# Softmax attention feeding a gated FFN on one core: key rests shared by four heads, and batch 0 begun with 384 of its 448 queries

## The chip, the core and the metric

The kernel runs on one core of one Trainium2 chip. The metric is the device time of one execution in microseconds (us). A core has TensorE (PE: products; PEld is its loading of the stationary operand), VectorE (DVE), ScalarE (ACT: here exponential, tanh and copies), GpSimd (POOL: here casts, and the issue of the loads that turn float32 into float16) and SyncE (SP: the issue of other transfers). TensorE writes into PSUM, which has eight banks; the other data lie in SBUF. One row of a tile is one partition.

## What is computed

Cut from the reference:

```python
batch, n_heads, seq, head_dim = (8, 12, 448, 64)

def _attn_ref(q, k, v):
    scale = 1.0 / np.sqrt(q.shape[-1])
    scores = scale * np.matmul(q, k.transpose(0, 1, 3, 2))
    scores = scores - np.max(scores, axis=-1, keepdims=True)
    attn = np.exp(scores)
    attn = attn / (np.sum(attn, axis=-1, keepdims=True) + 1e-09)
    return np.matmul(attn, v).astype(np.float32)

def _moe_ref(x, w_gate, w_val, w_out):      # x: (3584, 768), d_ff: 1536
    g = x @ w_gate
    silu = g * (1.0 / (1.0 + np.exp(-g)))
    val = x @ w_val
    return (silu * val @ w_out).astype(np.float32)

# x = attn_out.transpose(0, 2, 1, 3).reshape(B * S, H * D)
```

All inputs and the output are float32; the kernel works in float16 with float32 sums.

## The kernel before

Heads are taken in pairs, 48 in all, six to a batch of 448 queries. Three things are woven together: the attention of one pair (scores, exponential, product with the values), the first FFN layer of a block whose attention is complete ("gate" and "value" products, 12 groups of 6 + 6 a block), and the second FFN layer of the block before. A block is 384 queries (even blocks) or 512 (odd ones); two blocks make two batches. The whole kernel is put into a fixed order by hand (`manual_schedule`), and each engine executes its part in that order.

The 448 keys of a pair lie in four chunks of 112. For a chunk, the scores of both heads are two products with 64 rows each, in the two row halves of TensorE; the result, keys by queries, goes into one score tile of two banks:

```python
ps_s = ...tile_pool(name="ps_s", bufs=3, space=PSUM)    # 3 tiles of two banks
ps_f = ...tile_pool(name="ps_f", bufs=2, space=PSUM)    # 2 tiles of one bank

def qk(pr, c):
    t = qkT[pr]
    s = ps_s.tile([128, 2, 512], FP32, tag="s")
    for hx in range(2):
        nc.tensor.matmul(
            s[:, hx, 0:S],
            lhsT=t[ts(hx, 64), c * P : c * P + 128],
            rhs=t[ts(hx, 64), ds(S + (1 - hx) * D, S)],
            start=True, stop=True)
    e = Es[pr % NE][:, ds(c * EB, 16)].rearrange("p (h b) x -> p h (b x)", h=2)
    nc.scalar.activation(e[:, :, 0:S], s[0:P, :, 0:S], AF.Exp, scale=sm_scale)
```

The product with the values uses blocks of 128 queries as the stationary operand and 64 values plus a column of ones (for the sum) as the moving one, 8 products a chunk, 32 a pair. Queries 384 to 447 of the two heads share one block (`a7[:, 6]`). The seven blocks of a pair fit one bank of `ps_f`. DVE then takes the reciprocal of the sums and multiplies.

```python
def pv_chunk(pr, c):
    if c == 0:
        accs[pr] = ps_f.tile([128, 512], FP32, tag="f", name="acc")
    ...
    for j in range(3):
        for hx in range(2):
            nc.tensor.matmul(a7[:, 2 * j + hx],
                lhsT=e[:, ds(c * EB + 9 * hx + 2 * j, 2)].rearrange(...),
                rhs=vo[:, hx, c, 0 : D + 1], ...)          # 112 rows, 65 columns
    for hx in range(2):
        nc.tensor.matmul(a7[:, 6], ..., rhs=vo[:, hx, c, 0 : D + 1], ...)
    if c < NC - 1:
        return
    nc.vector.reciprocal(r[:, 0:7], a7[:, :, D])
    nc.vector.tensor_tensor(xt[:, 0:n], a7[:, 0:n, 0:D], r[...], ALU.mult)
    ...
```

Q and K must be turned so that the 64 features lie along the rows. For the first 11 pairs TensorE does it (products with a unit matrix, then a DVE copy, `turn`); for the others POOL casts and a DMA transpose turns. The attention results must be turned too (`turn_x`): on TensorE for the first 12 pairs, in a bank of `ps_f` or in the accumulator's own, by DMA transposes for the others.

The start is a loop over the 24 chunks of batch 0, in which no FFN product can run yet. The `dummy` products here and there work on zeros; they only keep TensorE running.

```python
for u in range(FIRST * NC):                 # 6 pairs x 4 chunks
    pr, c = divmod(u, NC)
    qk(pr, c)
    if u == 1:
        dummy(1); turn(); dummy(1)
    ...
    elif u >= 6 and c == 2:
        prep(pr + 2)()                      # q and k of a later pair
    if c == 1:
        for w in wq.pop(pr, []):            # loads; first FFN weights with pair 0
            emit(w)
    if u in CAT: copy_v(...)
    if u in XAT: turn_x(...)
    for _ in range(...):
        if u >= 5 and pieces[0][0] * NC + pieces[0][1] <= u - 3:
            piece()                         # pv_chunk of an earlier chunk
```

After that comes the body, a list of steps: two or three chunks of scores, the products with the values for one pair, then as many FFN groups as are due.

```python
for x, (chunks, todo) in enumerate(plan):
    for pr, c in chunks:
        qk(pr, c)
    ...
    for _, p0 in todo:
        pv(p0)                              # 4 chunks, 32 products
    ...
    for y in range(nf): run_fv()            # gate 6, tanh, value 6
    for _ in range(no): run_o()             # second layer: 12 products
    ...
    while turns:
        turn_x(turns.pop(0))
```

A gate group takes a score tile of `ps_s`, a value group and a second-layer group a bank of `ps_f`. The last part of the output is evicted in two halves of 192 columns:

```python
for ch, oh in steps:
    last = last_block and ch == n // 128 - 1
    ...
    if last and oh:
        parts = [(OH, OH // 2), (OH + OH // 2, OH // 2)]
```

Of the kernel before, what the change touches and what calls it, by code (L numbers as in the profile page):

```python
# [19 lines left out]
NPE = 11  # L20
# [3 lines left out]
WIDE = 8  # L24
XPE = 12
NE = 4
NX = 6
NV = 5
VS = 9
EB = 15  # L30
# [3 lines left out]
def kernel(  # L34
# [24 lines left out]
    MQ = S - D  # L59
# [13 lines left out]
    load_table("exp_and_others")  # L73

# [7 lines left out]
    ps_f = ctx.enter_context(tc.tile_pool(name="ps_f", bufs=2, space=PSUM))  # L82

    Es = [consts.tile([P, NC * EB + 1, D], FP16, name=f"E{i}") for i in range(NE)]
    Xts = [consts.tile([128, 7, D], FP16, name=f"xt{i}") for i in range(NX)]
    Xrs = [consts.tile([D, 128], FP16, name=f"xr{i}") for i in range(3)]
    Vts = [consts.tile([P, 2, NC, D + 2], FP16, name=f"vo{i}") for i in range(NV)]
    vraw = consts.tile([P, VS, 2, NC, D], FP16, name="vraw")
# [11 lines left out]
    wo = [consts.tile([128, NFB, OH], FP16, name=f"wo{i}") for i in range(2)]  # L100
# [5 lines left out]
    def dummy(n):  # L106
        wp = ps_f.tile([128, 512], FP32, tag="f", name="wp")
        for _ in range(n):
            nc.tensor.matmul(wp[:], lhsT=warm[:, 0:128], rhs=warm[:], start=True, stop=True)  # L109

    def load_qk32(pr):
        rq = raws.tile([P, 2, NC, D], FP32, tag="rq", bufs=RB)
        rk = raws.tile([P, 2, NC, D], FP32, tag="rk", bufs=RB)
        for dst, src in ((rq, q), (rk, k)):
            nc.sync.dma_start(dst[:], src[0, 2 * pr : 2 * pr + 2].rearrange("h (p c) d -> p h (c d)", c=NC))
        raw[pr] = (rq[:], rk[:])
# [3 lines left out]
    def load_qk16(pr, n=2):  # L120
        h0 = 2 * (pr % 2) if pr >= 14 else 0
        if h0 == 0:
            q16 = raws.tile([P, 4, NC, D], FP16, tag="rq", bufs=RB, name="q16")
            k16 = raws.tile([P, 4, NC, D], FP16, tag="rk", bufs=RB, name="k16")
            pairbuf[:] = [q16, k16]
        q16, k16 = pairbuf
        for dst, src in ((q16, q), (k16, k)):
            flat = src.rearrange("b h s d -> (b h) s d")[2 * pr : 2 * pr + 2 * n]
            nc.gpsimd.dma_start(dst[:, ds(h0, 2 * n)], flat.rearrange("h (p c) d -> p h (c d)", c=NC))  # L129
        for i in range(n):  # L130
            h = h0 + 2 * i
            raw[pr + i] = (q16[:, h : h + 2], k16[:, h : h + 2])

    def load_v(pr, n=1):
        b, h = divmod(2 * pr, H)
        nc.gpsimd.dma_start(  # L136
            vraw[:, ds(pr % VS, n)].rearrange("p r h c d -> p (r h) (c d)"),
            v[b, h : h + 2 * n].rearrange("h (p c) d -> p h (c d)", c=NC),
        )
# [4 lines left out]
    def load_w(kind, i):  # L144
        if kind == "o":
            src = moe_w_out[:, ts(i, OH)].rearrange("(f p) m -> p f m", p=128)
            dst = wo[i]
        else:
            src = (moe_w_gate if kind == "g" else moe_w_val)[:, ts(i, DF // 4)].rearrange(
                "(t a p) m -> t p a m", p=128, t=2  # L150
            )
            for t in range(2):
                nc.gpsimd.dma_start(wgv[kind, i][:, ts(t, NCB // 2), :], src[t])
            return
        nc.gpsimd.dma_start(dst[:], src)

    def prep(pr):
        rq, rk = raw[pr]
        if pr == 0 or pr >= NPE:
            qk16 = attp.tile([P, 2, NC, 2, D], FP16, tag="qk16", bufs=3)  # L160
            for t, src in enumerate((rq, rk)):
                dst = qk16[:, 1 - t].rearrange("p c h d -> p h c d")
                if pr == 0:
                    nc.vector.tensor_copy(dst[:, 0], src[:, 0])
                    nc.scalar.activation(dst[:, 1], src[:, 1], AF.Copy)
                else:
                    nc.gpsimd.tensor_copy(dst, src)  # L167
        qkT[pr] = attp.tile([128, 2 * S + D], FP16, tag="qkT", name="qkT", bufs=5)
        if pr >= NPE:
            nc.sync.dma_start_transpose(  # L170
                qkT[pr][:, 0 : 2 * S].rearrange("p (c q) -> p c q", q=P),
                qk16[:].rearrange("p t c h d -> p (t c h d)"),
            )
            nc.sync.dma_start_transpose(
                qkT[pr][:, 2 * S :].rearrange("p (c q) -> p c q", c=1),
                qk16[0:D, 1, 0].rearrange("p h d -> p (h d)"),
            )
            return None

        def turn0():  # L180
            for t in range(2):
                tp = ps_s.tile([128, 2, 512], FP32, tag="s", name="tp")
                for c in range(NC):
                    for hx in range(2):
                        nc.tensor.matmul(
                            tp[ts(hx, 64), c // 2, ds(c % 2 * P, P)],
                            lhsT=qk16[:, 1 - t, c, hx],
                            rhs=ident[0:P, 0:P],
                            start=True,
                            stop=True,  # L190
                        )
                dst = qkT[pr][:, ts(1 - t, S)].rearrange("p (a x) -> p a x", a=2)
                nc.vector.tensor_copy(dst[:, 0], tp[:, 0, 0 : 2 * P])
                nc.scalar.activation(dst[:, 1], tp[:, 1, 0 : 2 * P], AF.Copy)
                if t == 0:
                    tq = tp
            nc.vector.tensor_copy(qkT[pr][:, 2 * S :], tq[:, 0, 0:D])

        def turn():
            if pr < FIRST + 2:  # L200
                tp = ps_s.tile([128, 2, 1024], FP16, tag="s", name="tp")[:, 0]
            else:
                tp = ps_f.tile([128, 1024], FP16, tag="f", name="tp")
            for i in range(2 * NC + 1):
                t, c = (1 - i // NC, i % NC) if i < 2 * NC else (0, 0)
                for hx in range(2):
                    src = raw[pr][t][:, hx, c, :]
                    nc.tensor.transpose(tp[ts(hx, 64), ts(i, P)], src, ident[0:P, 0:P])  # L208
            nc.vector.tensor_copy(qkT[pr][:], tp[:, 0 : 2 * S + D])  # L209

        return turn if pr else turn0

    def qk(pr, c):
        t = qkT[pr]
        s = ps_s.tile([128, 2, 512], FP32, tag="s")
        for hx in range(2):
            nc.tensor.matmul(  # L217
                s[:, hx, 0:S],
                lhsT=t[ts(hx, 64), c * P : c * P + 128],
                rhs=t[ts(hx, 64), ds(S + (1 - hx) * D, S)],  # L220
# [3 lines left out]
        e = Es[pr % NE][:, ds(c * EB, 16)].rearrange("p (h b) x -> p h (b x)", h=2)  # L224
        nc.scalar.activation(e[:, :, 0:S], s[0:P, :, 0:S], AF.Exp, scale=sm_scale)  # L225

    def qk_half(pr, half, between=None):
# [414 lines left out]
```

The softmax here doesn't subtract the row's maximum and nothing guards it: scores larger than these inputs give would overflow.

## Time and profile before

Three runs of the kernel before took 453.17, 453.20 and 453.62 us. The profiled execution has a span of 451.7 us; TensorE had a mean granted clock of 0.998 of full speed.

| stage | from, to (us) | what runs |
|---|---|---|
| start | 0 to 29.8 | attention of batch 0; loads of q, k, v and the first weights |
| body | 29.8 to 446.6 | FFN, with the attention of the other 42 pairs up to about 380 us |
| tail | 446.6 to 451.7 | last eviction and output |

| group | count | mean of one |
|---|---|---|
| exponential of a score tile, 2 x 448 columns (ACT) | 192 | 919 ns |
| tanh of a gate group, 384 / 512 columns (ACT) | 48 / 48 | 496 / 598 ns |
| gate and value products, 384 / 512 columns (PE) | 576 / 576 | 326 / 379 ns |
| second-layer products, 384 / 192 columns (PE) | 660 / 24 | 326 / 246 ns |
| score products, 448 columns on 64 rows (PE) | 384 | 355 ns |
| products with the values, 65 columns on 112 rows (PE) | 1536 | 193 ns |

How to read it: the page gives busy time by engine, then the span in 40 slices with a digit of tenths for each, then the chain of work that ended last. The durations of TensorE's products overlap[...]; the mean of one is therefore not its price. What a product costs in a row is the difference of the starts. A table of stretches of time shows which engine is full in which stage.

### The profile page before, as it was taken

Reading aid. Unit: us, or ns where it says so; the run is one execution under the profiler, and the core shown is the slowest. Engines: PE = TensorE matmul, PEld = TensorE weight load, DVE = VectorE, ACT = ScalarE, POOL = GpSimd, SP = SyncE. Lnnn points to the kernel's source line nnn. Section 1 sums busy time; section 2 is a strip of 40 time slices with the busy share of each in tenths; the row PEclk is TensorE's granted clock in tenths of the full one; section 3 lists DMA queues with packets and bytes.
Section 4 is the critical chain, followed back from the end, with each engine's and each line's share of the span. In section 5 each row is a group of like instructions: output and inputs, shape, how many; then the busy total and the mean of one; then the engine's idle time right before and its main releaser. Section 6 shows DMA issues by size and latency. Waiting matters only on the chain.

```text
span 451.7 us, 9871 instructions
## 1 busy us (share of the span) xinstructions
PE 441.9 (98%) x4024; PEld 247.0 (55%) x4024; DVE 201.6 (45%) x447; ACT 238.8 (53%) x350; POOL 141.8 (31%) x228
## 2 busy tenths in 40 slices
PE   8999999999999999999999999999999999999995
PEld 3655565545455556454555656545455666544563
DVE  3666562456654434455443534353453544055300
ACT  6965666566746465554554546644555462222221
POOL 8755715927642225252313405330100000000000
PEclk9999999999999999999999999999999999999999
DMA  9999999999969379874749758772503112200033
GB/s 142 173 200 201 196 172 174 180 209 119 145 93 133 46 129 124 132 120 71 126 74 120 98 78 143 118 105 68 101 20 68 46 46 57 70 2 0 17 100 95
DMA packets 105101, 48.71 MB, mean 108 GB/s; under 512 B 59744, under 2 KB 101600, under 8 KB 105056
## 3 DMA queue, kind: packets, MB, share of 16 engines
q0 software_dynamic: 43392, 23.37, 41.2%
q1 hardware_dynamic: 61664, 24.71, 28.9%
q8 instruction: 31, 0.51, 0.5%
q14 instruction: 14, 0.11, 0.1%
HBM read 47.19 MB, written 11.01 MB: 129 GB/s over the span
## 4 chain that ended last, share of the span: by engine, by line
PE 93%; DVE 3%; ACT 2%; issue 1%; DVEq 0%; ACTq 0%
PE op L371 24%; PE gp L326 23%; PE vp L326 23%; PE s L217 9%; PE acc L243 9%; PE acc L251 2%; ACT E L225 2%; PE tp L208 1%; PE wp L109 1%; DVE t L345 1%; ACT sg L341 1%; DVE qkT L209 0%; DVE xt L264 0%; PE acc L291 0%; DVE hts L348 0%
## 5 line engine op out<-in xcount | busy, mean ns | idle before, releaser
L225 ACT ACTIVATE E<-s 112x896 f16<-112x896 f32 x192 | 162.1, 919 | 27.5 <-PE s L217 27.4
L326 PE MATMUL gp<-X,wg 128*128 128x384 f16 (+1 forms) x576 | 124.7, 352 | 0.0
L326 PE MATMUL vp<-X,wv 128*128 128x384 f16 (+1 forms) x576 | 124.6, 352 | 0.0
L371 PE MATMUL op<-wo,hts 128*128 128x384 f16 (+1 forms) x684 | 116.1, 323 | 0.0
L345 DVE SCALAR_TENSOR_TENSOR t<-sg,gp 128x384 f32<-128x384 f32 (+1 forms) x96 | 59.7, 621 | 121.8 <-ACT sg L341 121.8
L341 ACT ACTIVATE sg<-gp 128x384 f32<-128x384 f32 (+1 forms) x96 | 52.5, 547 | 84.8 <-PE gp L326 83.6
L371 PEld LDWEIGHTS <-hts 128*128 128x128 f16 x684 | 65.5, 98 | 45.9 <-issue 3.9
L326 PEld LDWEIGHTS <-wv 128*128 128x128 f16 x576 | 56.3, 98 | 52.6
L326 PEld LDWEIGHTS <-wg 128*128 128x128 f16 x576 | 53.1, 97 | 45.6 <-issue 1.1
L378 ACT ACTIVATE osb<-op 128x384 f32<-128x384 f32 (+1 forms) x57 | 27.8, 487 | 92.5 <-PE op L371 92.5
L167 POOL COPY qk<-q 112x512 f16<-112x512 f16 x37 | 22.9, 619 | 144.5 <-DMA qkT<-qk 143.1
L348 DVE SCALAR_TENSOR_TENSOR hts<-t,vp 128x384 f16<-128x384 f32 (+1 forms) x96 | 59.6, 621 | 10.0
L243 PEld LDWEIGHTS <-E 112*128 112x128 f16 x1152 | 46.7, 97 | 18.2 <-issue 17.5
L243 PE MATMUL acc<-vo,E 112*128 112x65 f16 x1152 | 53.0, 193 | 1.3 <-DVE vo L142 0.7
L217 PE MATMUL s<-qkT 64*128 64x448 f16 x384 | 50.6, 355 | 0.2
L251 PE MATMUL acc<-vo,E 112*128 112x65 f16 x384 | 42.9, 193 | 0.0
L262 DVE RECIPROCAL R<-acc 128x7 f32<-128x7 f32 x48 | 9.8, 205 | 70.6 <-PE acc L251 70.5
L129 POOL DMA_DIRECT2D k<-in_k_dram x44 | 29.0, 660 | 9.5 <-DMA wo<-in_moe_w_out_dram 7.8
L129 POOL DMA_DIRECT2D q<-in_q_dram x44 | 29.3, 666 | 5.2 <-PE s L217 2.5
L136 POOL DMA_DIRECT2D vraw<-in_v_dram x42 | 28.0, 666 | 8.4 <-DVE vo L142 7.2
L217 PEld LDWEIGHTS <-qkT 64*128 64x128 f16 x384 | 14.5, 94 | 25.8 <-issue 18.6
L264 DVE TENSOR_TENSOR xt<-acc,R 128x384 f16<-128x384 f32 (+1 forms) x48 | 27.6, 574 | 1.7
(41 smaller groups left out, 148.2 us busy)
## 6 DMA issues: line engine op xcount, KB each, us to landing
q<-in_q_dram POOLq DMA_DIRECT2D x41, 112.0 KB, 4.0
k<-in_k_dram POOLq DMA_DIRECT2D x41, 112.0 KB, 4.6
vraw<-in_v_dram POOLq DMA_DIRECT2D x39, 112.0 KB, 4.6
wg<-in_moe_w_gate_dram POOLq DMA_DIRECT2D x8, 288.0 KB, 10.1
wv<-in_moe_w_val_dram POOLq DMA_DIRECT2D x8, 288.0 KB, 10.2
wo<-in_moe_w_out_dram POOLq DMA_DIRECT2D x2, 1152.0 KB, 22.0
out_dram<-osb SPq DMA_DIRECT2D x8, 288.0 KB, 3.0
out_dram<-osb SPq DMA_DIRECT2D x8, 240.0 KB, 3.1
```

The source lines that it names most:

```text
L129: nc.gpsimd.dma_start(dst[:, ds(h0, 2 * n)], flat.rearrange("h (p c) d -> p h (c d)", c=NC))
L136: nc.gpsimd.dma_start(vraw[:, ds(pr % VS, n)].rearrange("p r h c d -> p (r h) (c d)"), v[b, h : h + 2 * n].rearrange("h (p c) d -> p h (c ...
L217: nc.tensor.matmul(s[:, hx, 0:S], lhsT=t[ts(hx, 64), c * P : c * P + 128], rhs=t[ts(hx, 64), ds(S + (1 - hx) * D, S)], start=True, stop=True,)
L225: nc.scalar.activation(e[:, :, 0:S], s[0:P, :, 0:S], AF.Exp, scale=sm_scale)
L243: nc.tensor.matmul(a7[:, 2 * j + hx], lhsT=e[:, ds(c * EB + 9 * hx + 2 * j, 2)].rearrange("p b x -> p (b x)"), rhs=vo[:, hx, c, 0 : D + 1] ...
L251: nc.tensor.matmul(a7[:, 6], lhsT=e[:, ds(c * EB + 6 + hx, 2)].rearrange("p b x -> p (b x)"), rhs=vo[:, hx, c, 0 : D + 1], start=False, st ...
L326: nc.tensor.matmul(dst[:, 0:n], lhsT=wslice(kind, fb, cb), rhs=X[kk][:, cb, ds(c0, n)], start=(cb == 0), stop=(cb == NCB - 1),)
L341: nc.scalar.activation(sg[:, 0:n], gp[:, 0:n], AF.Tanh, scale=0.5)
L345: nc.vector.scalar_tensor_tensor(t1[:, 0:n], sg[:, 0:n], 1.0, gp[:, 0:n], ALU.add, ALU.mult)
L348: nc.vector.scalar_tensor_tensor(hts[:, fb, 0:n], t1[:, 0:n], 0.5 * HS, vp[:, 0:n], ALU.mult, ALU.mult)
L371: nc.tensor.matmul(op[:, 0:w], lhsT=hts[:, fb, ts(ch, 128)], rhs=wo[oh][:, fb, ds(m0 - oh * OH, w)], start=(fb == 0), stop=(fb == NFB - 1),)
L378: nc.scalar.activation(osb[:, ds(m0, w)], op[:, 0:w], AF.Copy, scale=1.0 / HS)
```

## The change

The change does these things together:

- **Keys in three chunks of 128 and a rest of 64.** The rests of both heads of two neighbouring pairs (four heads) share one score tile: four products of 64 rows by 64 columns, one in each quarter of TensorE, then one exponential. Two pairs need 7 score tiles and 7 exponentials instead of 8. For this the loads lay out K and V so that the rest of one head comes in the lower and that of the other in the upper 64 rows.
- **Products with the values** are 4 blocks of queries for each head: 24 products on 128 rows and 8 on the 64 rows of the rests a pair (of the seventh query block, half the result columns are not used). Each head has a bank of its own, so a pair takes two.
- **Batch 0 first for 384 queries.** In the start, each of the six pairs is scored for 384 queries only, which are those of the first FFN block. Its other 64 queries are done for all heads in three score tiles (`qk_rest`, two at the end of the start, one after the first FFN group), one run of products (`pv_rest`) in the next step and one turn (`turn_rest`) in the step after.
- The order of the start is given by a string of letters; TensorE turns q and k for 14 pairs instead of 11 and the results for 18 instead of 12, now in score tiles. Every step of the body has three score tiles. The accumulator of the start has a PSUM pool of its own, given back before the first FFN group.
- q and k of pair 0 are issued by two engines; the second-layer weights come in four parts, later than before.

The core of the diff:

```diff
-NPE = 11
+NPE = 14
-XPE = 12
+XPE = 18
+Q1 = 384
+START = "sstdsdvsstsppppssvtsvppxppsstsppxpspsvtspsppvvpsxsppxpssptsppsppsxx"
 ...
     ps_s = ctx.enter_context(tc.tile_pool(name="ps_s", bufs=3, space=PSUM))
-    ps_f = ctx.enter_context(tc.tile_pool(name="ps_f", bufs=2, space=PSUM))
+    first_acc = ExitStack()
+    psum = {"a": first_acc.enter_context(tc.tile_pool(name="ps_a", bufs=1, space=PSUM))}
 ...
+    def low(pr, hx):
+        return hx == pr % 2
 ...
     def qk(pr, c):
-        t = qkT[pr]
         s = ps_s.tile([128, 2, 512], FP32, tag="s")
+        n = width(pr)                      # 384 for pairs 0 to 5, else 448
+        if c < KR:                         # KR = 3 full chunks
+            t = qkT[pr]
+            for hx in range(2):
+                nc.tensor.matmul(s[:, hx, 0:n], lhsT=t[ts(hx, 64), ts(c + low(pr, hx), 128)],
+                                 rhs=t[ts(hx, 64), ds(NC * 128, n)], start=True, stop=True)
+            e = Es[pr % NE][:, c]
+        else:                              # the rests of pairs pr and pr + 1
+            for hx in range(2):
+                for p in (pr, pr + 1):
+                    lo = low(p, hx)
+                    t = qkT[p]
+                    nc.tensor.matmul(s[ts(1 - lo, 64), hx, 0:n],
+                        lhsT=t[ts(hx, 64), ds(0 if lo else KR * 128 + 64, 64)],
+                        rhs=t[ts(hx, 64), ds(NC * 128, n)], start=True, stop=True)
+            e = Ers[pr // 2 % NR][:]
+        nc.scalar.activation(..., s[:, :, 0:n], AF.Exp, scale=sm_scale)
 ...
+    def pv_mm(pr, hx, c, j):
+        lo = low(pr, hx)
+        ...
+        if c < KR:
+            rows, e, col = slice(0, 128), Es[pr % NE][:, c], c + lo
+        else:
+            rows, e, col = (slice(0, 64), Ers[...], 0) if lo else (slice(64, 128), Ers[...], KR)
+        nc.tensor.matmul(accs[pr][0][hx][:, ts(j, D + 1)], lhsT=e[rows, ds(hx * S + j * 128, 128)],
+                         rhs=Vts[pr % NV][rows, hx, col, 0 : D + 1], ...)
 ...
+    def pv(pr, mid):
+        for hx in range(2):
+            for c in range(KR):
+                pv_piece(pr, c, (hx,))
+            if hx == 0:
+                mid()                      # turn_x of the pair before
+        pv_close(pr)
 ...
         if pr < XPE:
-            tp = accs[pr] if pr < FIRST else ps_f.tile([128, 512], FP32, tag="f", name="xtp")
-            for j in range(3):
+            tp = ps_s.tile([128, 2, 512], FP32, tag="s", name="xtp")[:, 0]
+            for j in range(slots(pr)):     # 3, or 4 from pair 6 on
 ...
                 while l < l0 + 128:
                     b, j = divmod(l, S)
-                    c, p0 = divmod((j + D) % S, P)
+                    n = S // NC
+                    c, p0 = divmod(j, n)
 ...
+                for pr, c in sorted(chunks, key=lambda x: -(x[1] == RU)):
+                    qk(pr, c)              # a shared rest first
+                for _, p0 in todo:
+                    pv_piece(p0, RU)       # then the 64-row products with the values
 ...
+                if x == 0:
+                    qk_rest(2)
+                elif x == 1:
+                    rest = pv_rest()
+                elif x == 2:
+                    turn_rest(rest)
```

## The prediction

> **What bounds the kernel now.** I read the page's shares and slices first, then the chain, then a table by stage, then the order of time in one step.
>
> ```profile
> PE 441.9 (98%) x4024; PEld 247.0 (55%) x4024; DVE 201.6 (45%) x447; ACT 238.8 (53%) x350; POOL 141.8 (31%) x228
> ...
> ACT  6965666566746465554554546644555462222221
> ...
> DMA  9999999999969379874749758772503112200033
> ...
> PE 93%; DVE 3%; ACT 2%; issue 1%; DVEq 0%; ACTq 0%
> ```
>
> TensorE is busy nearly everywhere and makes up 93% of the chain; ScalarE (ACT) is at half load on average, but near 0.9 in the second slice, and the DMA engines are full for the first 110 us. The averages hide stages, so the table of stretches (columns: length, then busy time and count for PE, PEld, DVE, ACT, POOL, then clock, DMA share, GB/s):
>
> ```profile
> 5.30:29.80 24.50, 22.52 (x396) 14.28 (x395) 14.05 (x33) 22.64 (x28) 17.58 (x26) 1.00 1.33 179
> 29.80:86.60 56.80, 55.54 (x638) 34.31 (x636) 28.24 (x60) 35.02 (x50) 32.50 (x50) 1.00 1.34 182
> 86.60:235.90 149.30, 149.07 (x1322) 79.40 (x1321) 73.18 (x162) 85.45 (x123) 60.69 (x100) 1.00 0.83 119
> 235.90:390.00 154.10, 154.10 (x1343) 87.35 (x1342) 67.41 (x156) 79.33 (x121) 26.86 (x44) 1.00 0.47 81
> ...
> 446.60:451.70 5.10, 0.00 (x0) 0.00 (x0) 0.00 (x0) 0.32 (x1) 0.00 (x0) 0.85 0.30 64
> ```
>
> There are two regimes. Up to 29.8 us (**the start**: only attention of batch 0) ACT is busy 22.64 of 24.50 us: the exponentials and TensorE bind together. From 29.8 to 446.6 us (**the body**) TensorE has next to no gap, and only its own work counts. The last 5.1 us are eviction and output. In the order of time, one step of the body:
>
> ```profile
> 199.30 1.14 PE L371 MATMUL op<-wo,hts 128*128 128x384 f16 x6
> 200.38 0.74 PE L217 MATMUL s<-qkT 64*128 64x448 f16 x6
> 201.05 0.35 PE L243 MATMUL acc<-vo,E 112*128 112x65 f16 x6
> ...
> 202.02 1.46 PE L326 MATMUL gp<-X,wg 128*128 128x512 f16 x6
> 203.32 0.38 PE L326 MATMUL vp<-X,wv 128*128 128x512 f16 x1
> ```
>
> Differences of starts are the true price (durations overlap). Six score products, two heads side by side, take 0.67 us for three chunks; the single starts are 190 ns apart by pairs, so 0.57 us is work and 0.10 us is lost before the next form. The six 384-column products before them (163 ns each, 0.98 us) start 1.08 us earlier: again 0.10 us. The 32 products with the values take 0.97 us, 30.3 ns each. Six 512-column products take 1.30 us, 216 ns each.
>
> **What the Trainium skill says.** "TensorEngine Tiling (Array Packing)", Key Properties: changing the tiling mode drains TensorE. That fits the 0.10 us at each entry and exit above. The same page, Restrictions and Gotchas: row tiles must write different PSUM banks; the score pairs here do. "TensorE: Matmul & The Clock Gate", Part 3, has products in different tiles start about 4 ns apart; the pairs of score products show 3 to 4 ns. The same page, Back-to-back issue gap, gives a floor of about 25 ns between starts; the trace disagrees within pairs: the 64-column turns of the rests (column pairs) come 4 ns and 28 ns apart in turn, so two tiles share one slot. No run yet shows this for 65-column products on 64 rows.
>
> **The change, part by part.** Counts are from the instruction order of both kernels, split at the first FFN product.
>
> *Start.* Three query blocks of batch 0 instead of three and a half: 18 full score tiles and 3 rest tiles of 768 columns replace 24 tiles of 896 (the old order pushed 2 more, of pair 6, in before the FFN). Eight old exponentials in a row took 6.65 us, 0.83 each. ACT needs 598 ns for 512 and 496 ns for 384 columns (the tanh rows), 0.80 ns a column, so a 768-column tile should take 0.83 - 0.10 = 0.73 us in a row. ACT before the last needed exponential: old 24 x 0.83 = 19.9 us, new 21 x 0.73 = 15.3 us, a gain of 4.6 us. Of the three deferred-rest tiles, two stand at the very end of the start and one after the first FFN step.
>
> TensorE in the start, old: scores 26 x 0.19 = 4.9, values 192 x 0.030 = 5.8, 7 turns of q and k (63 pairs at 0.048) 3.0, turns of the results 1.0, dummies 1.3, about 50 mode changes at 0.10 = 5.0; 21 us in the 24.5. New: scores 21 x 0.163 + two deferred-rest tiles of 0.22 = 3.9, values 108 x 0.030 + 18 pairs x 0.030 = 3.8, 6 turns (8 pairs at 0.029 + 4 at 0.048 = 0.43) 2.6, results 1.0, dummies 1.0, about 42 changes 4.2; 16.5 us. TensorE also sheds 4.5 us. Both binding engines shed the same, and the waits beside them (about 3 us of TensorE in the old start) I leave as they are. q and k of pair 0 now come over two queues instead of one (the old ones landed about 0.5 us apart), worth some 0.4 us, and POOL has four more issues ahead of the first weights, at 0.66 us each while it is busy 17.6 of 24.5 us, which I set against it. First FFN product: 29.8 - 4.6 = **25.2 us**.
>
> *Body.* The FFN is unchanged: 576 x 162.6 ns + 576 x 215.8 + 672 x 162.6 = 327.2 us (the old kernel's 24 halves of 192 columns at 82.5 make the same). The rest:
> - Scores: 166 chunk pairs become 126 full units plus 21 shared rests, in which four 64x64 products run together: 147 x 0.19 = 27.9 against 31.5: **-3.6 us**.
> - Values: 1344 products at 30.4 ns (40.9 us) become 1044 full ones (31.7) and 348 of 64 rows, in pairs on two row halves and two banks: 174 x 0.030 = 5.3. **-3.9 us**, if they pair.
> - Mode changes: 119 become 144, because a shared rest needs a mode of its own and seven more q/k turns each bring three: +25 x 0.10 = **+2.5 us**.
> - Turns of q and k: three pairs (27 x 0.048 = 1.3) become seven (7 x 0.43 = 3.0): **+1.7 us**.
> - Turns of the results on TensorE instead of by DMA: 18 products and two batches of rests (1.4 us) become 36 x 0.056 + 18 short ones at 0.028 = 2.5: **+1.1 us**.
> - The deferred rest tile: **+0.2 us**.
>
> Sum: -2.0 us. DVE and POOL are at or below 60% of every stretch of the body; their changes cost nothing by themselves.
>
> *New waits in the body.* Result turns and q/k turns now take score tiles (three, two banks each), and both accumulator banks are taken by one pair. In a plain step this fits: the first exponential is done some 1.3 to 1.6 us after the scores begin, and the gate product wants its tile at about 1.75 us. In the 12 steps for pairs 6 to 17 a result turn asks for that tile at about 1.3 us and the next user asks for the second tile (free at 2.1 to 2.4 us) at about 1.9. That is 0 to 0.6 us a step; I take 0.12: **+1.4 us**.
>
> *Tail.* A variable n reused in the output loop makes the "last" test false, so the final 384 columns are evicted whole (0.49 us against 0.33) and written as two large transfers instead of four small ones issued in a row. These about cancel: +0.1 us.
>
> Sum: 453.2 - 4.6 - 2.0 + 1.4 + 0.1 = **448.1 us**.
>
> **Rivals.**
> 1. *The first weights gate the start.* Gate and value weights of the first quarter are issued at 12.8 to 15.8 us and land about 10 us later, near 25 us, with the DMA engines full; with later issues they may come at 26.5. For: the full DMA row. Against: the bytes ahead of them are the same. Total about 449.5.
> 2. *Score tiles become the bound.* If every one of the 12 steps loses 0.6 us, and the seven with a q/k turn another 0.3, the body costs 8 us more than I book for it: about 455. For: ACT still spends 2.5 us on three tiles in a row. Against: early steps have no output eviction in ACT's queue, and the total ACT work falls by 10%.
> 3. *The 64-row products don't pair.* Then values cost 1392 x 30.4 ns, 5.3 us more: about 453, no gain. For: the weight loads may be the limit at 65 columns (29 ns apart in the old trace). Against: the two row halves' weights load 4 ns apart in the score pairs.
> 4. *The order of the start is better packed* and recovers the 3 us of waits too: about 445.
>
> **Range and chances.** Rivals 1 and 2 in part are likely, 3 I give one in five, 4 one in six. Range 444.5 to 452.5. Over 2% faster means under 444.1, which needs rival 4 and no new waits: 0.09. Slower by 2% means over 462: 0.02. Predicted: 448.1 us, faster 0.09, same 0.89, slower 0.02.
>
> **What would show it.** Right: the first FFN product near 25 us; 21 exponentials of about 0.82 us each; four shared-rest products starting within some 12 ns and costing one 190 ns slot; rest products with values at 15 ns on average; tanh and FFN rows unchanged; the body near 416 us. Wrong: TensorE idle on an exponential before the gate or a result turn of over 0.2 us a step (rival 2); the first gate or value product waiting for its weights (1); eight rest products taking 0.24 us (3). A mode change dearer than 0.10 us around 64x64 tiles would also spoil the sum: there are some 60 of them.

## The result and the profile after

The changed kernel takes **457.78 us** (457.62 to 457.90), beside 453.31 us for the kernel before in the same rounds: ratio 1.0097, 95% interval 1.0080 to 1.0115. It is 1.0% slower, and the predicted range ended at 452.5 us. The profiled execution has a span of 456.0 us (before: 451.7).

The page after, busy time and chain:

```profile
PE 441.8 (97%) x4211; PEld 249.6 (55%) x4211; DVE 205.5 (45%) x471; ACT 219.3 (48%) x328; POOL 178.8 (39%) x298
...
PE 86%; ACT 6%; DVE 3%; issue 2%; POOL 2%; DMA 1%; DVEq 0%; ACTq 0%; POOLq 0%
```

TensorE's busy time is the same to 0.1 us in a span 4.3 us longer, ScalarE has shed 19.5 us of work, and yet other engines now hold more of the chain (TensorE 93% before, 86% now). Work has become waiting. Where, the table of stretches says (length, then busy time and count for PE, PEld, DVE, ACT, POOL, then clock, DMA share, GB/s):

```profile
5.30:25.58 20.28, 18.64 (x402) 12.42 (x399) 13.03 (x31) 17.70 (x25) 15.48 (x24) 1.00 1.29 178
25.58:50.00 24.42, 21.82 (x332) 13.67 (x330) 13.96 (x35) 14.11 (x20) 15.35 (x22) 1.00 1.34 201
50.00:85.00 35.00, 34.03 (x432) 20.54 (x432) 21.87 (x54) 20.85 (x29) 23.06 (x38) 1.00 1.34 168
...
110.00:240.00 130.00, 129.31 (x1169) 72.19 (x1169) 55.53 (x130) 66.91 (x101) 60.99 (x103) 1.00 0.80 112
240.00:395.00 155.00, 153.89 (x1380) 88.50 (x1379) 66.32 (x155) 73.96 (x115) 34.82 (x59) 1.00 0.50 79
```

The start ends at 25.58 us instead of 29.79. But in the next 24.42 us TensorE is idle for 2.60, in the 35 us after that for 0.97, and even in the two long stretches behind for 0.69 and 1.11; before, it was idle for 0.23 us in the stretch from 86.60 to 235.90 and for none from 235.90 to 390.00. No other engine is busy for more than 0.7 of any stretch of the body, except GpSimd while it issues loads (85 to 110 us, not shown): this does not look like a second engine becoming full, but like an order of use.

For the sum I took every difference of starts between single products of the trace. Products of 384 columns come 162.6 ns apart and those of 512 columns 215.8, so a column costs 1/2.4 ns. What a difference has above its columns is work up to 0.03 us, and otherwise a **pause**; where the mode changes (other rows or columns of the array), up to 0.13 us above is booked as the price of the change, and the rest as a pause. The body is from the first FFN product to the last product:

| us | before | after | difference | predicted |
|---|---|---|---|---|
| start, to the first FFN product | 29.79 | 25.58 | -4.2 | -4.6 |
| body: scores | 32.04 | 28.75 | -3.3 | -3.4 |
| body: products with the values | 40.9 | 38.25 | -2.65 | -3.9 |
| body: turns of q and k | 1.4 | 3.45 | +2.05 | +1.7 |
| body: turns of the results | 1.46 | 2.52 | +1.05 | +1.1 |
| body: FFN, both layers | 327.2 | 326.9 | -0.3 | 0 |
| body: changes of mode | 11.83 (119) | 14.61 (144) | +2.8 | +2.5 |
| **body: pauses** | **1.79** | **10.6** | **+8.8** | **+1.4** |
| tail | 5.4 | 5.35 | 0 | +0.1 |

(The deferred rest's predicted +0.2 is set to the scores here.) One row is wrong, and it decides. The pauses of the changed kernel by what stands ahead and behind: 3.96 us inside the products with the values, 2.72 between the score chunks of a step, 0.87 from scores to values, 0.85 from values to the gate product, 0.71 ahead of second-layer groups, 0.49 and 0.44 ahead of turns, 0.36 from turns of q and k to the gate product, the rest small. Taken by the instruction whose end released TensorE, as the trace names it, ScalarE's exponentials hold 4.8 us of them, VectorE's `hts` 3.3 and its `t` 1.1 (the two passes over an FFN group), the copy of the deferred rest's turn 0.8, and ScalarE's eviction of output 0.7. The same step that the prediction showed of before, now in the order of time on TensorE (L469 gate and value, L258 scores, L371 values; brackets: idle time and what ended it):

```profile
235.22 1.46 PE L469 MATMUL gp<-X,wg 128*128 128x512 f16 x6
236.51 1.46 PE L469 MATMUL f<-X,wv 128*128 128x512 f16 x6
237.90 0.74 PE L258 MATMUL s<-qkT 64*128 64x448 f16 x6
238.48 0.19 PE L371 MATMUL f<-vo,er 64*128 64x65 f16 x1
238.88 0.28 PE L371 MATMUL f<-vo,er 64*128 64x65 f16 x7 [0.21 <-DVE hts L491]
239.09 0.91 PE L371 MATMUL f<-vo,E 128*128 128x65 f16 x24
```

One product with a rest starts and the second, which belongs to the other head and so to the other bank, comes 0.40 us later. VectorE over the same time:

```profile
237.34 0.69 DVE L488 SCALAR_TENSOR_TENSOR t<-sg,gp 128x512 f32<-128x512 f32 x1 [1.11 <-ACT sg L484]
238.14 0.69 DVE L491 SCALAR_TENSOR_TENSOR hts<-t,f 128x512 f16<-128x512 f32 x1
```

`hts` reads the value group's bank until 238.83 us. A pair now needs both single banks of PSUM for its products with the values; one was the bank of this value group. The value products end at about 237.97 us, 0.86 us before that, and the three score chunks between fill only 0.58 us. This stands in 11 steps, each of them behind one that ended with a value group; they hold 3.3 of the 3.96 us. The rest is 0.04 us in each of 18 steps, where the bank comes from a second-layer group that ScalarE evicts. Before, a pair took one bank, and no pause stands inside its products with the values.

The first steps, without products for values yet, and one late one show the other kinds:

```profile
29.21 0.37 PE L258 MATMUL s<-qkT 64*128 64x448 f16 x2 [0.59 <-ACT er L306]
...
35.70 0.37 PE L258 MATMUL s<-qkT 64*128 64x448 f16 x2 [0.78 <-ACT er L279]
...
40.13 0.37 PE L258 MATMUL s<-qkT 64*128 64x448 f16 x2 [0.66 <-DVE X L354]
...
372.85 0.30 PE L371 MATMUL acc<-vo,er 64*128 64x65 f16 x8 [0.71 <-ACT E L279]
```

At 29.21 the step's third score tile waits until the third tile of batch 0's deferred rest has had its exponential, which was put ahead of the step's own three tiles: four users of three tiles. At 40.13 the fourth user is the rest's turn (L354 copies it out). At 372.85 the accumulator itself is a score tile and has to wait for an exponential.

### The profile page after: what moved, and what is told of

It reads as the page before. It is cut to its first block, busy times and chain, and to the rows that moved or that the text cites. A ratio compares the mean times of both kernels' runs of the same rounds, so it can differ in the third digit from the quotient of the medians.

```text
span 456.0 us, 10303 instructions
## 1 busy us (share of the span) xinstructions
PE 441.8 (97%) x4211; PEld 249.6 (55%) x4211; DVE 205.5 (45%) x471; ACT 219.3 (48%) x328; POOL 178.8 (39%) x298
## 4 chain that ended last, share of the span: by engine, by line
PE 86%; ACT 6%; DVE 3%; issue 2%; POOL 2%; DMA 1%; DVEq 0%; ACTq 0%; POOLq 0%
PE f L514 24%; PE f L469 23%; PE gp L469 22%; PE f L371 8%; PE s L258 5%; ACT E L279 3%; DVE t L488 1%; PE s L271 1%; DMA k<-in_k_dram 1%; DVE hts L491 1%; ACT sg L484 1%; PE acc L371 1%; PE tp L244 1%; POOL vraw L122 1%; ACT er L279 1%
## 5 line engine op out<-in xcount | busy, mean ns | idle before, releaser
L279 ACT ACTIVATE E<-s 128x896 f16<-128x896 f32 (+1 forms) x144 | 120.8, 910 | 9.1 <-PE s L258 9.0
L469 PE MATMUL f<-X,wv 128*128 128x384 f16 (+1 forms) x576 | 124.7, 353 | 0.0
L514 PE MATMUL f<-wo,hts 128*128 128x384 f16 x672 | 116.0, 326 | 0.4 <-DVE t L488 0.4
L469 PE MATMUL gp<-X,wg 128*128 128x512 f16 (+1 forms) x522 | 113.5, 354 | 0.4
L488 DVE SCALAR_TENSOR_TENSOR t<-sg,gp 128x512 f32<-128x512 f32 (+1 forms) x87 | 54.2, 624 | 87.4 <-ACT sg L484 87.4
L484 ACT ACTIVATE sg<-gp 128x512 f32<-128x512 f32 (+1 forms) x87 | 47.9, 551 | 90.4 <-PE gp L469 89.3
L469 PEld LDWEIGHTS <-wv 128*128 128x128 f16 x576 | 56.2, 98 | 52.9 <-DVE xt L418 0.2
L521 ACT ACTIVATE osb<-f 128x384 f32<-128x384 f32 x56 | 27.4, 490 | 113.6 <-PE f L514 109.7
L469 PEld LDWEIGHTS <-wg 128*128 128x128 f16 x576 | 53.7, 98 | 45.8 <-issue 0.7
L491 DVE SCALAR_TENSOR_TENSOR hts<-t,f 128x384 f16<-128x384 f32 (+1 forms) x96 | 59.6, 621 | 10.0
L258 PE MATMUL s<-qkT 64*128 64x448 f16 (+1 forms) x288 | 38.6, 350 | 2.5 <-ACT er L279 0.8
L371 PEld LDWEIGHTS <-E 128*128 128x128 f16 x1116 | 37.6, 97 | 3.1 <-issue 0.5
L371 PE MATMUL f<-vo,E 128*128 128x65 f16 x960 | 37.8, 194 | 0.0
```

The costliest lines, as they stand in the source:

```text
L258: nc.tensor.matmul(s[:, hx, 0:n], lhsT=t[ts(hx, 64), ts(c + low(pr, hx), 128)], rhs=t[ts(hx, 64), ds(NC * 128, n)], start=True, stop=True,)
L279: nc.scalar.activation(e[:, 0 : 2 * S].rearrange("p (h q) -> p h q", h=2)[:, :, 0:n], s[:, :, 0:n], AF.Exp, scale=sm_scale)
L371: nc.tensor.matmul(accs[pr][0][hx][:, ts(j, D + 1)], lhsT=e[rows, ds(hx * S + j * 128, 128)], rhs=Vts[pr % NV][rows, hx, col, 0 : D + 1], ...
L469: nc.tensor.matmul(dst[:, 0:n], lhsT=wslice(kind, fb, cb), rhs=X[kk][:, cb, ds(c0, n)], start=(cb == 0), stop=(cb == NCB - 1),)
L484: nc.scalar.activation(sg[:, 0:n], gp[:, 0:n], AF.Tanh, scale=0.5)
L488: nc.vector.scalar_tensor_tensor(t1[:, 0:n], sg[:, 0:n], 1.0, gp[:, 0:n], ALU.add, ALU.mult)
```

## The experiments

All were timed in five rounds beside the kernel before (453.3 to 453.7 us there). Parts of the body as in the table above; ratio to the kernel before with its interval:

| run | us | ratio (95%) | first FFN at | work | pauses |
|---|---|---|---|---|---|
| before | 453.3 | | 29.79 | 402.9 | 1.8 |
| after | 457.78 | 1.0097 (1.0080 to 1.0115) | 25.58 | 399.9 | 10.6 |
| e1_whole | 456.11 | 1.0052 (1.0034 to 1.0070) | 27.30 | 398.2 | 9.3 |
| e3_rests | 456.79 | 1.0071 (1.0053 to 1.0090) | 25.34 | 399.8 | 9.5 |
| e4_erlast | 462.51 | 1.0196 (1.0175 to 1.0217) | 25.52 | 400.0 | 7.8 |
| e5_xpe12 | 455.36 | 1.0041 (1.0029 to 1.0053) | 25.09 | 398.7 | 9.6 |
| e6_npe12 | 455.99 | 1.0053 (1.0034 to 1.0072) | 25.66 | 398.9 | 10.7 |
| e7_wide0 | 457.40 | 1.0081 (1.0065 to 1.0098) | 25.80 | 399.9 | 10.4 |
| e8_copy | 458.14 | 1.0091 (1.0074 to 1.0108) | 25.44 | 399.8 | 10.8 |
| e9_mix | 451.10 | 0.9937 (0.9920 to 0.9954) | 27.30 | 396.0 | 7.1 |
| e10_nocopy | 452.39 | 0.9973 (0.9964 to 0.9982) | 27.37 | 396.0 | 8.2 |
| e11_early | 450.78 | 0.9926 (0.9910 to 0.9942) | 27.15 | 396.0 | 6.7 |
| e12_half | 450.32 | 0.9915 (0.9899 to 0.9931) | 28.70 | 396.1 | 5.0 |

Seven of these kernels have the same order of the start as the changed kernel or are that kernel itself (after, e3_rests to e8_copy), and their first FFN product comes at 25.09 to 25.80 us. A total thus carries some 0.7 us of chance in the start, and small gains are better read in the work and pauses of the body.

My theory: the loss is PSUM. All eight banks are in use (three score tiles of two, two single ones), the change has given them more users in a step, and TensorE waits for whoever still reads. The rivals: the loss lies in the added small work and changes of mode themselves; or in the split of batch 0; or ScalarE's run of three exponentials in a row sets the pace, whatever the banks. The letters A, B and C in the expectations stand for the theory and its rivals as they were put for that run.

### The split of batch 0 taken back: e1_whole

```diff
-Q1 = 384
+Q1 = 448                              # start on all 448 queries
-START = "...pssptsppsppsxx"
+START = "...pssptsppppxx"             # without the two tiles of the rest
-        return KR if pr < FIRST else KR + 1
+        return KR + 1                  # query blocks of a pair
-                if x == 0: qk_rest(2)
-                elif x == 1: rest = pv_rest()
-                elif x == 2: turn_rest(rest)
```

> The changed kernel with batch 0 done whole in the start (448 queries, no deferred rests). Theory A (the body lost its gain to waits for PSUM; some 3.2 us of them are in the three steps after the start, where the deferred rests take score tiles): the start gets 4 to 5 us longer (first FFN product near 30 us instead of 25.6), the body gets some 5.5 us shorter (3.2 us of waits and 2.3 us of rest work), so about 456.5 to 457.5 us: the split was worth nothing. Theory B (the body got slower by the work and mode changes added, not by waits): the split is a net gain of 2 us or more, so about 460 us.

The first FFN product came at 27.30 us, only 1.7 later than in the changed kernel; I had looked for about 30. So of the 4.2 us that the start gained, 1.7 come from the split, and 2.5 from all else that the change does there: the shared key rests (three exponentials fewer), the order of letters and the loads, which no run takes apart. The body became 3.4 us shorter: 1.7 of work, 0.4 of changes of mode, 1.3 of pauses. The split costs 1.7 us net. But its pauses did not all go with it; without the deferred rest the same early steps show a new one, ahead of the turn of q and k:

```profile
30.85 0.44 PE L244 MATMUL tp<-ident,k 64*64 64x64 f16 x16 [0.69 <-ACT E L279]
...
34.99 0.44 PE L244 MATMUL tp<-ident,k 64*64 64x64 f16 x16 [0.54 <-ACT er L279]
```

### The deferred rest moved to other places: e3_rests

```diff
+                if x == 1: rest = pv_rest()        # ahead of the FFN groups
+                elif x == 2: turn_rest(rest)
                 for y in range(nf):                # two groups in the first step
                     run_fv()
+                    if x == 0 and y == 0: qk_rest(2)   # between them
-                if x == 0: qk_rest(2)
-                ...
```

> The changed kernel with the deferred rests placed otherwise: a second FFN group behind the third rest tile in the first step, and the product and the turn of the rests ahead of the FFN group of their steps instead of behind it. Same work, same products. Theory A: of the 3.2 us that TensorE waits for score tiles between 29 and 41 us at most 1 us is left, total about 455 to 455.5 us. Theory B: same work, same time, 457.8 us within 0.5.

Pauses between score chunks fell from 2.72 to 0.19 us, as meant. The gain was 1.0 us and not 2.5 (the intervals of the two kernels just overlap; the sum of pauses fell from 10.6 to 9.5), because the wait turned up at the next user of a score tile (0.49 to 1.29 us ahead of the q/k turns) and, by 0.3 us, inside the products with the values:

```profile
31.25 0.44 PE L244 MATMUL tp<-ident,k 64*64 64x64 f16 x16 [0.63 <-ACT E L279]
...
36.96 0.44 PE L244 MATMUL tp<-ident,k 64*64 64x64 f16 x16 [0.59 <-DMA k<-in_k_dram]
```

The second line names a load of k. But the exponential of the step's first score tile runs from 35.99 to 36.91 us in this trace, and the turn at the same place in e1_whole names that exponential; I read the tile as what held, and no run took the load alone apart.

### The 64-row products put last: e4_erlast

```diff
-                for _, p0 in todo:
-                    pv_piece(p0, RU)   # directly behind the scores, same mode
 ...
+        pv_piece(pr, RU)               # behind the 128-row products of both heads
         pv_close(pr)
```

> The changed kernel with the 64-row products with the values behind the 128-row ones instead of ahead of them. The second head's bank is then needed some 0.4 us later, but two more mode changes fall in each of 42 pairs (84 x 0.10 = 8.4 us). Theory A: the 4.0 us that TensorE stands between two of the first rest products, waiting for the bank that the last value group of the FFN still holds, fall to under 0.8 us; total 457.8 + 8.4 - 3.5 = about 462.5 us. Theory B (those pauses are not waits for the bank): they stay, about 466 us.

462.51 us, where the account gave 462.5. The pauses inside the products with the values vanished (3.96 to 0): the first head's 12 products are now ahead of the second head's bank. 77 more changes of mode cost 7.2 us, and the pauses ahead of the result turn, which waits for an exponential because it takes a score tile, grew from 0.44 to 3.0 us:

```profile
59.89 0.54 PE L371 MATMUL f<-vo,E 128*128 128x65 f16 x12
60.59 0.36 PE L446 MATMUL xtp<-ident,xt 128*128 128x128 f16 x4 [0.16 <-ACT E L279]
60.78 0.53 PE L371 MATMUL f<-vo,E 128*128 128x65 f16 x12
61.24 0.29 PE L371 MATMUL f<-vo,er 64*128 64x65 f16 x8
```

That the total came out to 0.01 us is luck: 8.4 was booked for the changes of mode and 3.5 for the pauses, and 7.2 and 2.8 came. The run confirms the price of a change of mode (7.2 us for 77, 0.094 each) and shows that more than half of the time not spent on the bank was spent on the tile.

### Fewer turns on TensorE: e5_xpe12 and e6_npe12

```diff
-XPE = 18
+XPE = 12      # e5_xpe12: results of 12 pairs turned on TensorE, as before
```

```diff
-NPE = 14
+NPE = 12      # e6_npe12: q and k of 12 pairs
```

> The changed kernel with the results of pairs 12 to 17 turned by DMA again (as the kernel before does), so that six turns on TensorE and six uses of a score tile go. Theory A (waits for PSUM on top of work): 1.2 us of products and some 0.9 us of pauses around those turns and the gate products behind them go, total about 455.7 us. Theory B (only work counts): 456.6 us. Theory C (the DMA engines, full in the first 100 us, are why the turns were moved): the second FFN block waits for its input, 458 us or more.

> The changed kernel with q and k of pairs 12 and 13 turned by DMA (TensorE turns 12 pairs instead of 14). Each turn costs 0.69 us with its mode changes, and 0.2 us is lost before the gate product behind it. Theory A: 457.8 - 1.4 - 0.2 to 0.4 = about 456.1 us. Theory B: 456.4 us. Theory C: TensorE waits for the turned q and k of these pairs near 65 to 75 us, 458 us or more.

The totals came near theory A in both: 455.36 (expected 455.7) and 455.99 us (456.1). In e5_xpe12 the body bears it out: 1.2 us of work and 1.0 of pauses are gone. In e6_npe12 it doesn't: 1.0 of work and 0.7 of changes of mode went, but the sum of pauses stayed (10.7 against 10.6; 0.2 less behind the q/k turns, 0.3 more ahead of other gate products). That is theory B, and the 0.3 us between the two forecasts are too little to tell by the total. These additions of the change cost some 4 us together and brought nothing: handed back to the other way of turning, the same work showed no new wait of its size.

### The accumulators of pairs not taken from score tiles: e7_wide0

```diff
-WIDE = 2
+WIDE = 0
```

> The changed kernel with the last two pairs' accumulators in two single banks like all others, instead of a score tile. Theory A: the single wait of 0.87 us near 373 us (the fourth tile asked of three) goes, a bank wait of 0 to 0.4 us comes, total 457.1 to 457.5 us. Theory B: no change beyond 0.2 us.

The time is 457.40 us, with an interval that overlaps the changed kernel's. The wait of 0.87 us at 372.85 is gone. In the next step with values one of some 0.6 us has come, for a single bank that the eviction of output (L521) still reads (sum of pauses 10.4 against 10.6):

```profile
379.18 0.20 PE L371 MATMUL f<-vo,er 64*128 64x65 f16 x1
379.82 0.28 PE L371 MATMUL f<-vo,er 64*128 64x65 f16 x7 [0.44 <-ACT osb L521]
```

### The value bank freed early: e8_copy

In the steps that end with a value group ahead of a pair's products, ScalarE copies that bank to SBUF, so that VectorE no longer holds it.

```diff
             group("v", vp)
+            if vcopy[0]:
+                vs = fp.tile([128, 512], FP32, tag="sg", name="vs")
+                nc.scalar.activation(vs[:, 0:n], vp[:, 0:n], AF.Copy)
+                vp = vs
```

> The changed kernel in which ScalarE copies the value group out of PSUM in those steps that end with a value group and are followed by products with the values (about 14 copies of 0.5 to 0.6 us), so that the bank is free about 0.7 us after the group instead of about 1.0 us; VectorE reads the copy. Theory A (the second accumulator waits for that bank): the pauses between the first rest products fall from 4.0 us to 1 to 1.8 us, total about 455.2 us. Theory B (not the bank), or ScalarE's copies push the exponentials back so that score tiles are waited for instead: 457.5 to 458.5 us.

The bank is what held: the pause inside the products with the values fell from 3.96 to 1.24 us, of which 0.7 are the small ones behind the eviction, and of the 11 steps only 3 still have as much as 0.175 us between the first two starts. Theory A was right about the bank, theory B about the time, which did not fall: 458.14 us. ScalarE's three exponentials now start behind the copy, and their users wait: ahead of the result turn 0.44 to 2.08, ahead of the gate product 0.85 to 1.50, ahead of the q/k turn 0.03 to 0.49. The sum of pauses is 10.8 against 10.6. One step in which both halves can be seen:

```profile
60.07 0.35 PE L371 MATMUL f<-vo,er 64*128 64x65 f16 x8
60.35 0.54 PE L371 MATMUL f<-vo,E 128*128 128x65 f16 x12
60.95 0.36 PE L445 MATMUL xtp<-ident,xt 128*128 128x128 f16 x4
61.14 0.53 PE L371 MATMUL f<-vo,E 128*128 128x65 f16 x12
```

The eight rest products run on, and then 12 products that take 0.37 us in the changed kernel (60.41 to 60.78) are followed by the turn only after 0.60.

### All of it together: e9_mix and e10_nocopy

e9_mix is e1_whole with `XPE = 12`, `NPE = 12`, `WIDE = 0` and the copies; e10_nocopy is the same without the copies.

> All of it together: batch 0 whole in the start, results turned on TensorE for 12 pairs, q and k for 12 pairs, no score tile as an accumulator at the end, and the copies of the value groups. Theory A, if the parts add: 456.1 - 2.1 - 1.7 - 0.4 - 2.6 = about 449.3 us, under the kernel before (453.3). Theory B (work alone): about 452.5 us. Theory C: 455 us or more, the loads bind.

> The mixed version without ScalarE's copies of the value groups. In the changed kernel the copies only moved the pauses from the accumulator's bank to the score tiles of the turns and gate products. Theory A: with fewer turns on TensorE the same exchange is nearly even: pauses between the first rest products 1.9 back to about 4 us, those behind the products with the values 2.0 down to under 1 us, total 451 to 452.3 us. Theory B: the copies did all of what the mix gained over its parts: 453.5 us.

451.10 us: 0.6% faster than the kernel before, and between the 449.3 of parts that add and the 452.5 of work alone. Without copies it is 452.39, and the two intervals do not meet, so here the copies do help: the pauses inside the products with the values are 1.90 against 4.89 us, those behind the exponentials 1.98 against 0.42. That they help here and not in e8_copy fits with the six result turns gone, which waited longest there; no run took that alone apart.

What carries this version is not the body. Its length is 416.7 us against 416.5 before: 6.9 us less work, 1.7 more changes of mode, 5.35 more pauses. The gain is the 2.5 us of the start. The pauses that the change brought are only in part gone, so no run shows the body with its saved work and the old pauses.

### The q/k turn ahead of the scores: e11_early

```diff
+                if not todo and chunks and x + 6 < NPE:
+                    prep(x + 6)()          # steps without products for values
                 for pr, c in sorted(chunks, ...):
                     qk(pr, c)
```

> The mixed version in which the two steps without products with the values (the first two after the start) turn q and k ahead of their score products, so that the turn doesn't ask for the tile of an exponential that has just begun. Theory A (the two pauses of 0.85 and 0.70 us are waits for a score tile behind ScalarE): 0.6 to 1.1 us less, about 450.3 us. Theory B (they wait for loads of q and k): 451.1 us, no change.

450.78 us, lowest of those that leave nothing out, though its interval overlaps e9_mix's. The forecast gain did not come where it was looked for: the 1.29 us ahead of those two turns went, and 1.31 more came between the score chunks, now the fourth user of three tiles. The sum of pauses fell by 0.4 us, between gate and value products:

```profile
33.80 0.38 PE L271 MATMUL s<-qkT 64*64 64x448 f16 x4
34.12 0.36 PE L258 MATMUL s<-qkT 64*128 64x448 f16 x2
35.20 0.36 PE L258 MATMUL s<-qkT 64*128 64x448 f16 x2 [0.71 <-DVE qkT L245]
```

### Half of ScalarE's exponentials left out: e12_half

From pair 6 on, only one head's exponential is computed (the second head's are left out); everything else is e9_mix. This asks how much of the pauses is ScalarE's own pace.

```diff
+        nh = 1 if pr >= FIRST else 2
-        ...[:, :, 0:n], s[:, :, 0:n], AF.Exp, scale=sm_scale
+        ...[:, 0:nh, 0:n], s[:, 0:nh, 0:n], AF.Exp, scale=sm_scale
```

> The mixed version with exponentials of the first head alone from pair 6 on (448 of 896 columns; what the second head's products read is left from batch 0). It leaves out half of ScalarE's exponentials and nothing on TensorE. Theory A: what is left of pauses in the body of the mix (7.1 us) is mostly the burst of three exponentials in a row holding score tiles, and falls to 2.5 to 4 us; total about 447 to 448.5 us. Theory B (banks held by VectorE and mode changes): 450 us or more.

ScalarE's busy time fell from 223.9 to 171.4 us and the kernel by 0.8 us, to 450.32 (the intervals overlap):

```profile
PE 437.7 (98%) x4091; PEld 245.7 (55%) x4091; DVE 199.7 (45%) x461; ACT 171.4 (38%) x337; POOL 182.5 (41%) x303
```

Pauses between values and gate or turns (1.98 us) are all gone, and those between scores and q/k turns fell from 1.29 to 0.55. What stays is 1.90 inside the products with the values, 0.99 ahead of second-layer groups, 0.59 between gate and value groups, and one new pause where VectorE holds the tile:

```profile
71.23 0.36 PE L258 MATMUL s<-qkT 64*128 64x448 f16 x2
72.44 0.55 PE L258 MATMUL s<-qkT 64*128 64x448 f16 x4 [0.85 <-DVE hts L497]
```

The body is 2.1 us shorter, so the columns left out of ScalarE's exponentials account for about 2 of the 7 us of pauses (2.7 by the places that went); what the remaining columns hold the run can't say. By the instruction that released it, what stays is 1.4 us behind the eviction of output, 1.0 behind `hts`, 1.0 behind `t`, 0.6 behind ScalarE's copies, 0.5 behind exponentials and 0.3 behind a load of weights. The amount of ScalarE's work alone can't be the loss: the kernel before has 19.5 us more of it than the changed kernel, and 1.8 us of pauses. The start of this profile is 1.4 us later than e9_mix's, with the same work in it; why was not settled, so I compare the bodies.

## Why the prediction was wrong

- **Start: right.** Predicted 25.2 us, measured 25.58. The 21 exponentials are there, at 0.70 us each in a row (three take 2.21 us, the last of them 0.81) and not 0.73. The prediction's own sum holds two parts, three exponentials fewer (3 x 0.83 = 2.5 us) and narrower tiles from the split (21 x 0.10 = 2.1); e1_whole shows 2.5 for all but the split and 1.7 for the split, though the order and the loads changed with the first part. What was too high was my expectation for e1_whole, which gave the split the whole gain.

```profile
L279 ACT ACTIVATE E<-s 128x768 f16<-128x768 f32 x18 | 13.6, 813 | 1.9 <-PE s L258 1.8
L279 ACT ACTIVATE er<-s 128x768 f16<-128x768 f32 x3 | 2.4, 805 | 0.0
```

- **Scores, turns, FFN, tail: right** within 0.4 us each (first table). The four products of a shared rest start 3 to 4 ns apart and cost one slot of 190 ns.
- **Values: right in kind, 1.25 us short.** Full products came 31.0 ns apart instead of 30.4 (1044 of them: 0.6 us), and rest products cost 17.1 ns each instead of 15 (348: 0.7 us): they start 15 ns apart on average, but the last of each eight is counted with all its 27 ns. They do run in pairs; rival 3 is out.
- **Changes of mode: right** (+2.8 for +2.5). Leaving 64x64 for 64 rows costs 0.119 us, not 0.10. The Trainium skill ("TensorEngine Tiling (Array Packing)", Key Properties) has the drain but no price; here it is 0.09 to 0.12 us.
- **New waits in the body: the step that failed.** Booked at 0.12 us in 12 steps, 1.4 us; measured 8.8. At the places that it timed, the result turn and the gate product behind the values, 1.3 us came (0.44 and 0.85), in fewer and larger waits than 0.12 in each of 12 steps; the size is in part luck. What it left out is the rest. The prediction said itself that "both accumulator banks are taken by one pair", and then went on to time only the score tiles. The bank that the value group of the step before leaves to VectorE was not timed at all; pauses inside the products with the values are the largest single place (3.96 us, 3.3 of them behind that bank), shown by the releaser in the trace, and by e4_erlast and e8_copy, which took all or most of it away. The second place, between score chunks, is 2.72 us, 2.5 of them in the three first steps with score products: I gave the deferred rest +0.2 us as work and did not ask whose tile it takes.
- **Rival 2** had the direction and nearly the time (455), for a partly other reason. It looked for TensorE idle on an exponential before the gate product or a turn; in the changed kernel that is 1.8 us (0.85, 0.49 and 0.44), and only two steps lose over 0.2 us at a result turn. With the scores' own waits for tiles (2.72 and 0.87) and 0.36 behind q/k turns, the score tiles hold some 5.7 us of pauses, the single banks some 4.7. Rivals 1 and 4 did not come: no first gate or value product waits for its weights, and the start is not shorter than predicted.

Each wait taken away appeared in part at the next user of PSUM: e3_rests, e4_erlast, e7_wide0, e8_copy and e11_early all show it. The Trainium skill puts the matter in a line ("Trainium Kernel Development and Optimization", Best Practices): "TensorE tiling speeds up compute but not PSUM evacuation". The trace agrees: the change makes scores and values 6 us cheaper on TensorE, and VectorE's reading of a value group takes 621 ns as before (first line before, second after). The 8.8 us by which the pauses grow are not due to the tiling alone: the deferred rest and the turns in score tiles have their part.

```profile
L348 DVE SCALAR_TENSOR_TENSOR hts<-t,vp 128x384 f16<-128x384 f32 (+1 forms) x96 | 59.6, 621 | 10.0
L491 DVE SCALAR_TENSOR_TENSOR hts<-t,f 128x384 f16<-128x384 f32 (+1 forms) x96 | 59.6, 621 | 10.0
```

What is open: how much of the 5 us of pauses left in e12_half another order of the steps could save, and whether the pauses can be brought back to the 1.8 us of before at all; no run got below 5.0.

## What to carry to other kernels

Where TensorE has next to no gap and all PSUM banks are in use, write down for each step which tile each user takes, who reads it last and when, before booking a saving; a change that makes a unit smaller but takes two banks for one can lose more than it saves. Test a term by moving it alone: the totals for the turns were forecast to 0.4 us, and the split, which made the start 1.7 us shorter, cost 1.7 us net. A wait that goes at one place is a gain only when the sum of the pauses falls, so sum them over the whole body and don't look at the place that was mended.

## What was not expected of the hardware

- Products of 65 columns on 64 rows, in pairs on the two row halves and two banks, start 15 ns apart on average (107 ns from the first to the eighth in e4_erlast, where no pause falls between them). The Trainium skill ("TensorE: Matmul & The Clock Gate", Back-to-back issue gap) has a floor of about 25 ns between starts; between different tiles the starts come closer here.
- The price of a change of mode depends on where it goes (medians of the changed kernel): 0.094 to 0.098 us between full and 64-row products, 0.096 into 64x64 from full, 0.119 from 64x64 to 64 rows.
- A full product of 65 columns comes every 31.0 ns in the changed kernel (128 rows) and every 30.4 before (112 rows); no run shows whether the rows are the reason.
